# Block sums, weight sums and silu on other units, x added to the output by DMA, and another product order in an FNet and GLU kernel

## Chip, core and metric

One core of a Trainium2 chip. The metric is the time of one execution in device microseconds; of the kernel before there are three runs, median 832.66 us (832.14 to 834.09).

## What is computed

```python
x = A_x                                   # (1, 2048, 512), float32
xn = _layernorm(x, axis=-1)
# s: real part of a 2-D DFT of xn
a = jnp.einsum("bsd,ed->bse", xn, dft_hid_re)
b = jnp.einsum("bsd,ed->bse", xn, dft_hid_im)
s = jnp.einsum("ts,bse->bte", dft_seq_re, a) - jnp.einsum("ts,bse->bte", dft_seq_im, b)
# g: silu of a gated linear unit of xn, width 1792
h = _sigmoid(xn @ w_gate) * (xn @ w_up)
g = _silu(h @ w_down)
return x + s * g
```

## The kernel before

All large arrays are float32. A product of two float32 operands is made of three matmuls (`mm3`, lines 69 to 72): each operand is split into a high and a low half, and high x high (L70), high x low (L71) and low x high (L72) are summed in a PSUM bank. `split` (lines 65 to 67) makes the halves: ScalarE (ACT) copies the high one (L66), VectorE (DVE) subtracts it for the low one (L67). Every operand that TensorE (PE) reads thus costs one ACT and one DVE operation over 128 x 1024 elements.

The DFT along the sequence and that along the hidden axis are written as products of 2 x 2 blocks in seven products in place of eight. They need sums of blocks of the operands, and the seven products, numbered 1 to 7, are added up into blocks in a given order; `CHAIN` names the accumulator that a product goes on with (a, b or c), `ORDER` is the order of the products, (1, 5, 6, 3, 7, 2, 4). Sums of operand blocks are made on DVE by `combine` (L118).

All on-chip data lies in 53 equal pages of 128 x 1024 floats (`page`). The work is a list of *units* that is written out by hand. `add` puts a unit at the end of the list; `sooner(n, f)` runs f ahead of unit n, `after(n, f)` behind it. The loop at lines 979 to 991 walks the list: at unit n it first does what `sooner` has for n, then starts the loads of the units n to n+5, then makes the splits of the units n to n+2, then the unit's matmuls, then what `after` has for n. Each engine works its instructions off in that order, so this list fixes what is queued behind what on DVE, ACT, SyncE (SP, which issues loads) and GpSimd (POOL, which issues stores).

Three stages follow each other. The first (to about 425 us) makes the layer norm, the gate and up products, and most of the down products; it sums g into `g_part` in DRAM by accumulating DMAs (`gather`, L295). The change does not touch it.

The second is the product along the sequence, `seq_units`, with four columns of the result, `tc_` 0 to 3 (called column 0 to 3 below). A column has 28 units, one for each product and each of four parts `pp`; units 0 to 3 are the first product in `ORDER`, 4 to 7 the next, and so on. (Column 0 has eight units of the first stage's last down products between them.) A unit is 12 matmuls of 128 x 128 by 128 x 512. Behind the last part of a product, `after_product` copies an accumulator to a page (`snap`, ACT, L787) or joins it with a page (`join`, DVE, two operations, L794); the joins stand behind units 15, 19 and 23. The halves of an even column are stored to `f_part` (L763). The operand sums that products 5, 6, 7 and 4 need are made by `onto`, three units ahead: units 1 to 8, 13 to 16 and 21 to 24. Into this stage three kinds of work are put that later stages need:

- *block sums*: in the odd columns, `total` reads back what the even column stored (`first`), makes four sums of it and the new blocks (L118), and stores them to `f_part` (L779). For half 0 they stand behind units 20 to 23, for half 1 behind 28 to 31, that is behind units 0 to 3 of the next column or of the third stage.
- *weight sums*: four sums of the blocks of the hidden DFT's weights, `sums_ahead(n + 64, diffs, ...)`, behind units 3, 5, 6 and 8 of column 2 (DVE, L118; stored at L682).
- *silu*: `silu_ahead`, eight pages of g: load, sigmoid (ACT, L720), product (DVE, L118 called from L717), store to `gs_part` (L717), one every seven units from the end of column 0.

The third stage is the product along the hidden axis, `hidden_units`: two pairs of columns, seven products of two units each (27 units, since the very last product is one unit, `run_last`). The weights' splits are spread by hand over the units ahead (lines 851 to 855). Behind the product that ends a block (`BLOCK`: 3, 7, 2, 4), `give` multiplies it with the silu page, adds x (L882), and POOL stores it to the output (L884). `run_last` does the last block in three pieces, with products and sums on DVE (L923, L924) and stores by SP (L926); its last two pieces share one PSUM bank.

Of the kernel before, what the change touches and what calls it, by code (L numbers as in the profile page):

```python
# [12 lines left out]
ADD, SUB = ALU.add, ALU.subtract  # L13
# [18 lines left out]
def fnet_glu_kernel(ctx: ExitStack, tc: tile.TileContext, x, x_t, c_re, c_im, w_h, w_gu, w_down, out):  # L32
# [99 lines left out]
    def after(n, f):  # L132
        extra.setdefault(n, []).append(f)
# [537 lines left out]
            (b21.load, b21, b22, ADD, to[3]),  # L671
        ]

    def sums_ahead(n, make, blocks, to):

        steps = make(*blocks, to)

        def step(dst, a, b, op, to):
            at = dst()
            a, b = a.get(), b.get()  # L680
            combine(at, a, b, op)
            nc.gpsimd.dma_start(to, at)  # L682

        for i, v in enumerate(blocks):
            sooner(n + i // 2, v.load)
        for i, v in enumerate(steps):
            after(n + (3, 5, 6, 8)[i], lambda v=v: step(*v))

    def onto(a, b, op, engine, swap=False):

# [16 lines left out]
        return ops  # L707

    ORDER = (1, 5, 6, 3, 7, 2, 4)
    SLOT = {1: 0, "a": 0, 2: 1, "b": 1, 3: 2, 5: 3, 7: 4, 6: 5, 4: 6}  # L710

    def silu_ahead(n, i):
# [10 lines left out]
    def seq_units(job):  # L723
        ops = a_operands()
        left = waiting + [(job, k) for k in SEVEN]
        n = len(units)
        sums_ahead(n + 64, diffs, [Load(w_h[i, j], [4, D // 2]) for i in range(2) for j in range(2)], w_part)
        for i in range(NS // 2):
            silu_ahead(n + 28 + 7 * i, i)
        for q in range(2):  # L730
            sooner(n - 5 + q, ops[1, q].load)
            sooner(n - 3 + q, ops[1, q].get)
        for tc_ in range(NT):
            n = len(units)
            bop = {}
            for pp in range(4):
                b11, b12, b21, b22 = c_blocks(tc_, pp)
# [17 lines left out]

            first = {(half, j): Load(f_part[tc_ // 2, half, SLOT["ab"[j]]], [2, SB]) for half in range(2) for j in range(2)}

            def after_product(k, tc_=tc_, ps=ps, s=s, made=made, first=first):
                def put(blk):
                    half, j = blk // 2 ^ 1, blk % 2  # L760
                    to = f_part[tc_ // 2, half]
                    if tc_ % 2 == 0 or j:
                        nc.gpsimd.dma_start(to[SLOT["ab"[j] if tc_ % 2 == 0 else 3]], made[blk])  # L763
                    if tc_ % 2 == 0 or j == 0:
                        return
                    a0, b0 = (first[half, j].load() for j in range(2))
                    a1, b1 = made[blk - 1], made[blk]
                    t2 = []

                    def total(k):  # L770
                        if k == 6:
                            t2.append(page([2, SB], F32))
                        v = {
                            5: lambda: combine(a0, a0, a1, ADD),
                            7: lambda: combine(a1, a1, b1, ADD),
                            6: lambda: combine(t2[0], a0, b1, ADD),
                            4: lambda: combine(b0, t2[0], b0, ADD),
                        }[k]()
                        nc.gpsimd.dma_start(to[SLOT[k]], v)  # L779

                    for i, k in enumerate((5, 7, 6, 4)):
                        after(now[0] + 1 + i, lambda k=k: total(k))

                def snap(name, ch):
                    s[name] = page([2, SB], F32)
                    for d in range(2):
                        nc.scalar.activation(s[name][:, d, :], ps[ch, d], AF.Copy)  # L787
                    return s[name]

                def join(blk, name, ch, op, swap=False):  # L790
                    made[blk] = v = s[name]
                    for d in range(2):
                        x, y = v[:, d, :], ps[ch, d]
                        nc.vector.tensor_tensor(v[:, d, :], *((y, x) if swap else (x, y)), op=op)  # L794
                    put(blk)

                if k == 1:
                    snap("u1", "a")
                elif k == 5:
                    snap("u5", "c")  # L800
                elif k == 6:
                    snap("u2", "a")
                elif k == 3:
                    join(2, "u2", "c", SUB)
                elif k == 7:
                    join(3, "u5", "a", SUB, swap=True)
                elif k == 2:
                    join(0, "u1", "b", ADD)
                else:
                    made[1] = snap("u4", "a")  # L810
                    put(1)
# [19 lines left out]

            for k in ORDER:
                for pp in range(4):
                    m = len(units)
                    if (tc_ or pp > 1) and k in bop["t", pp]:
                        sooner(m - 6, bop["t", pp][k].load)
                        sooner(m - 3, bop["t", pp][k].get)
                    add([ops[k, pp // 2], bop[k, pp]], lambda k=k, pp=pp, run=run: run(k, pp))
                    if tc_ % 2 and pp == 3 and k in (7, 4):
                        for j in range(2):  # L840
                            sooner(m - 5 + 2 * j, first[0 if k == 7 else 1, j].load)
                    if left and pp % 2:
                        last_down(*left.pop(0))


    def hidden_units():
# [1 line left out]
        v1, v3, v2, v4 = (Load(w_part[i], [4, D // 2]) for i in range(4))  # L848
        a11, a12, a22 = (Load(w_h[i, j], [4, D // 2]) for i, j in ((0, 0), (0, 1), (1, 1)))
        w = {}  # L850
        for i, (k, v) in enumerate({1: a11, 5: v1, 6: v2, 3: v4, 7: v3, 2: a12, 4: a22}.items()):
            w[k] = Parts([v], v.load, [4, D // 2])
            if i < 5:
                sooner(n - 26 + 5 * i, v.load)
                sooner(n - 22 + 5 * i, w[k].get)
        CHAIN = {1: "a", 6: "a", 7: "a", 4: "a", 2: "b", 5: "c", 3: "c"}
        BLOCK = {3: (0, 1), 7: (1, 1), 2: (0, 0), 4: (1, 0)}
        for pair in range(NT // 2):
            hp = {}
            for k in ORDER:  # L860
                for half in range(2):
                    v = Load(f_part[pair, half, SLOT[k]], [2, SB])
                    hp[k, half] = Parts([v], v.load, [2, SB])
            gl, xl = ({(i, t): Load(a[(2 * pair + t) * 2 + i], [2, SB]) for i in range(2) for t in range(2)} for a in (gs_part, x_t))
            ps, s = {}, {}

            def done(k, pair=pair, gl=gl, xl=xl, ps=ps, s=s):
                def snap(name, ch):
                    s[name] = page([2, SB], F32)
                    for d in range(2):  # L870
                        nc.scalar.activation(s[name][:, d, :], ps[ch, d], AF.Copy)

                def give(ch, name=None, op=None, swap=False):
                    i, t = BLOCK[k]
                    g, xv = gl[i, t].load(), xl[i, t].load()
                    r = s[name] if name else page([2, SB], F32)
                    for d in range(2):
                        a, b = r[:, d, :] if name else g[:, d, :], ps[ch, d]
                        nc.vector.tensor_tensor(r[:, d, :], *((b, a) if swap else (a, b)), op=op or ALU.mult)
                    if name:  # L880
                        nc.vector.tensor_mul(r, r, g)
                    nc.vector.tensor_add(r, r, xv)  # L882
                    to = out[i * D // 2 : (i + 1) * D // 2, (2 * pair + t) * SB : (2 * pair + t + 1) * SB]
                    nc.gpsimd.dma_start(to.rearrange("(d p) t -> p d t", p=P), r)  # L884

                if k == 1:
                    snap("u1", "a")
                elif k == 5:
                    snap("u5", "c")
                elif k == 6:  # L890
                    snap("u2", "a")
                elif k == 3:
                    give("c", "u2", SUB, swap=True)
                elif k == 7:
                    give("a", "u5", SUB)
                elif k == 2:
                    give("b", "u1", ADD)
                else:
                    give("a")

            def run(k, half, hp=hp, ps=ps, done=done, tags=({"a": "pd", "b": "a", "c": "c"}, {"a": "b", "b": "a", "c": "c"})[pair]):
                ch = CHAIN[k]
                if k in (1, 2, 5) and half == 0:
                    for d in range(2):
# [20 lines left out]
                    row, col = (2 * i + d) * P, (2 * pair + t) * SB  # L925
                    nc.sync.dma_start(out[row : row + P, col + at.start : col + at.stop], r[:, d, at])  # L926

            for k in ORDER:
                m = len(units)
                for half in range(2):  # L930
                    sooner(m + half - 8, hp[k, half].load)
                if k in BLOCK:
                    sooner(m - 5, gl[BLOCK[k]].load)
                    sooner(m - 4, xl[BLOCK[k]].load)
                if k == 4 and pair == NT // 2 - 1:
                    add([hp[k, 0], hp[k, 1], w[k]], run_last)
                    continue
                for half in range(2):
                    add([hp[k, half], w[k]], lambda k=k, half=half, run=run: run(k, half))
# [104 lines left out]
```

## Time and profile before

| | |
|---|---|
| median of three runs | 832.66 us (832.14 to 834.09) |
| the profiled execution | 833.4 us |
| its span, first to last instruction | 831.6 us |
| PE, DVE, ACT, POOL busy | 812.3, 652.4, 491.3, 135.4 us |
| granted TensorE clock | 1.00 throughout |
| DMA | 207.27 MB, 249 GB/s on average |

The rows below and in the prediction are read like this. A group or timeline row gives the line, the engine, the operation, the tiles (written <- read), the form, the count, and in brackets the idle time of the engine ahead of it with what ended it. A row of waits reads "who <- for whom: us in all, times, longest". A row of the table by stretches gives start and end, length, then busy time and number of instructions of PE, PEld (the weight loads), DVE, ACT and POOL, the granted clock, the share of DMA engine time and the rate in GB/s. The end of a matmul is modelled: one of 128 x 512 is shown with 0.39 us.

The transfers that matter for the change, with the median from issue to landing:

```profile
g_part<-page POOLq DMA_DIRECT2D x77, 512.0 KB, 8.2
...
f_part<-page POOLq DMA_DIRECT2D x28, 512.0 KB, 6.8
...
page<-in_x_t_dram SPq DMA_DIRECT2D x8, 512.0 KB, 10.4
page<-in_w_h_dram SPq DMA_DIRECT2D x7, 512.0 KB, 9.9
out_dram<-page POOLq DMA_DIRECT2D x7, 512.0 KB, 7.7
```

### The profile page before, as it was taken

The page shows a single profiled execution, that of the slowest core. Times are in us where ns is not written, and L with a number is a line of the kernel's source. Part 1 is how long each engine was busy: PE and PEld are TensorE (multiplying, and loading weights), DVE is VectorE, ACT ScalarE, POOL GpSimd, SP SyncE. Part 2 cuts the span into 40 slices and gives each one's busy share as a digit, 9 for nine tenths or more (in the row PEclk, how much of TensorE's full clock was granted, in tenths as well). Part 3 has the DMA queues.
Part 4 walks back from the last instruction along what each step waited for, and adds up shares of the span by engine and source line. Part 5 has one row for each costly group of instructions (what it writes and reads, how often), then busy time and mean ns, then how long its engine had stood idle before and what let it go on. Part 6 is the DMA issues. An engine that isn't in the chain of part 4 may idle for free.

```text
span 831.6 us, 10507 instructions
## 1 busy us (share of the span) xinstructions
PE 812.3 (98%) x3687; PEld 673.0 (81%) x3687; DVE 652.4 (78%) x821; ACT 491.3 (59%) x762; POOL 135.4 (16%) x207
## 2 busy tenths in 40 slices
PE   8899999999999999999999999999989999999997
PEld 7888888888878888888888888888768888878786
DVE  6798867757787867776787797878898767887957
ACT  4566555654677888788877774552545245446260
POOL 2142422321111112122121100001110000011101
PEclk9999999999999999999999999999999999999999
DMA  8259998799677888989999998268965743899952
GB/s 316 107 176 392 286 273 264 189 323 302 163 172 174 227 184 194 253 211 202 291 288 291 291 326 316 69 218 270 419 250 203 277 153 127 277 360 414 413 205 102
DMA packets 58357, 207.27 MB, mean 249 GB/s; under 512 B 6592, under 2 KB 6848, under 8 KB 58304
## 3 DMA queue, kind: packets, MB, share of 16 engines
q1 hardware_dynamic: 35136, 122.70, 40.8%
q0 software_dynamic: 23168, 83.90, 39.0%
q8 instruction: 29, 0.48, 0.2%
q14 instruction: 24, 0.20, 0.1%
HBM read 122.16 MB, written 84.41 MB: 248 GB/s over the span
## 4 chain that ended last, share of the span: by engine, by line
PE 73%; issue 13%; DVE 8%; DMA 3%; ACT 2%; POOL 1%; SPq 0%; DVEq 0%; POOLq 0%
PE pd L72 6%; PE pd L71 6%; PE pd L70 6%; PE ga L71 4%; PE ga L70 4%; PE ga L72 4%; PE ua L71 4%; PE ua L72 4%; PE ua L70 4%; DVE page L67 3%; PE gc L70 3%; PE gc L71 3%; PE gc L72 3%; PE uc L71 3%; PE uc L72 3%
## 5 line engine op out<-in xcount | busy, mean ns | idle before, releaser
L67 DVE TENSOR_TENSOR page<-page 128x1024 fp32r<-128x1024 f32 (+1 forms) x340 | 320.8, 977 | 116.5 <-ACT page L66 115.8
L66 ACT ACTIVATE page<-page 128x1024 fp32r<-128x1024 f32 (+1 forms) x340 | 275.9, 859 | 108.5 <-DVE page L118 92.6
L118 DVE TENSOR_TENSOR page<-page 128x1024 f32<-128x1024 f32 (+2 forms) x184 | 167.9, 933 | 7.3 <-DMA page<-xn_part 6.5
L291 ACT ACTIVATE page<-pd 128x512 f32<-128x512 f32 x154 | 89.5, 595 | 62.2 <-PE pd L72 58.9
L295 POOL DMA_DIRECT2D g_part<-page x69 | 60.2, 903 | 276.0 <-ACT page L291 200.1
L72 PE MATMUL pd<-page 128*128 128x512 f32 x242 | 94.3, 389 | 0.6 <-DVE page L67 0.6
L71 PE MATMUL pd<-page 128*128 128x512 f32 x242 | 94.3, 389 | 0.4 <-DVE page L67 0.4
L70 PE MATMUL pd<-page 128*128 128x512 f32 x242 | 94.2, 389 | 0.0
L70 PE MATMUL ga<-page 128*128 128x512 f32 x192 | 74.9, 390 | 0.8 <-ACT page L308 0.8
L71 PE MATMUL ga<-page 128*128 128x512 f32 x192 | 75.0, 391 | 0.4 <-DVE page L67 0.4
L72 PE MATMUL ga<-page 128*128 128x512 f32 x192 | 74.8, 390 | 0.0
L71 PE MATMUL ua<-page 128*128 128x512 f32 x192 | 74.7, 389 | 0.0
L70 PE MATMUL ua<-page 128*128 128x512 f32 x192 | 74.7, 389 | 0.0
L72 PE MATMUL ua<-page 128*128 128x512 f32 x192 | 74.7, 389 | 0.0
L71 PE MATMUL gc<-page 128*128 128x512 f32 x132 | 51.6, 391 | 2.3 <-DVE page L67 2.3
L72 PEld LDWEIGHTS pd<-page 128*128 128x128 f32 x242 | 45.4, 188 | 10.3 <-DVE page L67 0.9
L71 PEld LDWEIGHTS pd<-page 128*128 128x128 f32 x242 | 45.4, 188 | 10.3 <-DVE page L67 0.8
L70 PEld LDWEIGHTS pd<-page 128*128 128x128 f32 x242 | 45.4, 188 | 9.4
L70 PE MATMUL gc<-page 128*128 128x512 f32 x132 | 51.7, 392 | 0.0
L70 PE MATMUL uc<-page 128*128 128x512 f32 x132 | 51.4, 389 | 0.0
L72 PE MATMUL uc<-page 128*128 128x512 f32 x132 | 51.4, 389 | 0.0
L72 PE MATMUL gc<-page 128*128 128x512 f32 x132 | 51.4, 389 | 0.0
(135 smaller groups left out, 1355.5 us busy)
## 6 DMA issues: line engine op xcount, KB each, us to landing
g_part<-page POOLq DMA_DIRECT2D x77, 512.0 KB, 8.2
page<-in_c_re_dram SPq DMA_DIRECT2D x36, 512.0 KB, 5.3
page<-f_part SPq DMA_DIRECT2D x36, 512.0 KB, 7.7
page<-in_c_im_dram SPq DMA_DIRECT2D x34, 512.0 KB, 6.4
page<-in_w_gu_dram SPq DMA_DIRECT2D x28, 512.0 KB, 7.4
f_part<-page POOLq DMA_DIRECT2D x28, 512.0 KB, 6.8
page<-in_w_down_dram SPq DMA_DIRECT2D x14, 512.0 KB, 9.0
page<-xn_part SPq DMA_DIRECT2D x14, 512.0 KB, 7.8
```

Of the source, the lines that this page charges most:

```text
L66: nc.scalar.activation(hi, src, AF.Copy)
L67: nc.vector.tensor_tensor(lo, src, hi.bitcast(F32), op=SUB)
L70: nc.tensor.matmul(ps, ws[0], ms[0], start=first, stop=False, skip_group_check=go_on)
L71: nc.tensor.matmul(ps, ws[0], ms[1], start=False, stop=False, skip_group_check=go_on)
L72: nc.tensor.matmul(ps, ws[1], ms[0], start=False, stop=last, skip_group_check=go_on)
L118: (engine or nc.vector).tensor_tensor(dst, a, b, op=op)
L291: nc.scalar.activation(pg[:, o, :], po, AF.Copy, scale=float(sign))
L295: nc.gpsimd.dma_start(g_part[i], pg, accum_op=ADD)
```

## The change

- The weight sums move from column 2 (behind units 3, 5, 6, 8) to column 1 (behind units 9, 10, 11, 12), with their loads at units 6 and 7.
- The silu products move to behind units 17, 18 and 20 of column 1 and 17, 18, 20, 25 and 27 of column 2.
- The block sums of half 0 move from units 20 to 23 to units 25 to 28; those of half 1 from units 28 to 31 to units 37 to 40 behind column 1 (9 to 12 of column 2) and 32 to 35 behind column 3 (4 to 7 of the third stage). The halves stored before are read back four and three units ahead of them.
- The third stage takes its products in the order (1, 2, 6, 5, 3, 7, 4), with accumulators b and c in other banks. The splits of the weights of products 1, 2, 6, 5, 3 stand behind units 9, 11, 17, 18 and 20 of column 3.
- In the third stage x is no longer loaded and added on DVE, other than for the last block. POOL copies x into the output from DRAM to DRAM in columns 2 and 3, and the block is added to it by an accumulating DMA.

No matmul is added or taken away. The diff:

```diff
-    def sums_ahead(n, make, blocks, to):
+    def sums_ahead(n, make, blocks, to, at=(3, 5, 6, 8)):
...
-            at = dst()
-            a, b = a.get(), b.get()
-            combine(at, a, b, op)
-            nc.gpsimd.dma_start(to, at)
+            v = combine(dst(), a.get(), b.get(), op)
+            nc.gpsimd.dma_start(to, v)
...
-            after(n + (3, 5, 6, 8)[i], lambda v=v: step(*v))
+            after(n + at[i], lambda v=v: step(*v))
...
     ORDER = (1, 5, 6, 3, 7, 2, 4)
+    TURNED = (1, 2, 6, 5, 3, 7, 4)
...
-        sums_ahead(n + 64, diffs, [Load(w_h[i, j], [4, D // 2]) for i in range(2) for j in range(2)], w_part)
-        for i in range(NS // 2):
-            silu_ahead(n + 28 + 7 * i, i)
+        silu = {1: (17, 18, 20), 2: (17, 18, 20, 25, 27)}
+        later = iter(range(2 * NT))
...
         for tc_ in range(NT):
             n = len(units)
+            if tc_ == 1:
+                blocks = [Load(w_h[i, j], [4, D // 2]) for i in range(2) for j in range(2)]
+                sums_ahead(n + 6, diffs, blocks, w_part, (3, 4, 5, 6))
+            for i in silu.get(tc_, ()):
+                silu_ahead(n + i - 3, next(later))
...
-                    a0, b0 = (first[half, j].load() for j in range(2))
...
                     def total(k):
+                        a0, b0 = (first[half, j].load() for j in range(2))
...
+                    at = n + 25 if half == 0 else n + 28 + (9 if tc_ < NT - 1 else 4)
+                    for j in range(2):
+                        sooner(at - 4 + j, first[half, j].load)
                     for i, k in enumerate((5, 7, 6, 4)):
-                        after(now[0] + 1 + i, lambda k=k: total(k))
+                        after(at + i, lambda k=k: total(k))
...
-                    if tc_ % 2 and pp == 3 and k in (7, 4):
-                        for j in range(2):
-                            sooner(m - 5 + 2 * j, first[0 if k == 7 else 1, j].load)
...
-        for i, (k, v) in enumerate({1: a11, 5: v1, 6: v2, 3: v4, 7: v3, 2: a12, 4: a22}.items()):
+        for i, (k, v) in enumerate({1: a11, 2: a12, 6: v2, 5: v1, 3: v4, 7: v3, 4: a22}.items()):
             w[k] = Parts([v], v.load, [4, D // 2])
             if i < 5:
-                sooner(n - 26 + 5 * i, v.load)
-                sooner(n - 22 + 5 * i, w[k].get)
+                at = n - 28 + (9, 11, 17, 18, 20)[i]
+                sooner(at - 5, v.load)
+                after(at, w[k].get)
...
+        LAST = NT // 2 - 1, 4
+
+        def place_out(pair, i, t):
+            v = out[i * D // 2 : (i + 1) * D // 2, (2 * pair + t) * SB : (2 * pair + t + 1) * SB]
+            return v.rearrange("(d p) t -> p d t", p=P)
+
+        def put_x(pair, i, t):
+
+            nc.gpsimd.dma_start(place_out(pair, i, t), x_t[(2 * pair + t) * 2 + i])
+
         for pair in range(NT // 2):
             hp = {}
-            for k in ORDER:
+            for k in TURNED:
...
+            for i, k in enumerate(TURNED):
+                if k in BLOCK and (pair, k) != LAST:
+                    after(n - 52 + 24 * pair + 3 * i, lambda pair=pair, k=k: put_x(pair, *BLOCK[k]))
...
-                    g, xv = gl[i, t].load(), xl[i, t].load()
+                    g = gl[BLOCK[k]].load()
...
-                    nc.vector.tensor_add(r, r, xv)
-                    to = out[i * D // 2 : (i + 1) * D // 2, (2 * pair + t) * SB : (2 * pair + t + 1) * SB]
-                    nc.gpsimd.dma_start(to.rearrange("(d p) t -> p d t", p=P), r)
+                    nc.gpsimd.dma_start(place_out(pair, *BLOCK[k]), r, accum_op=ADD)
...
-            def run(k, half, hp=hp, ps=ps, done=done, tags=({"a": "pd", "b": "a", "c": "c"}, {"a": "b", "b": "a", "c": "c"})[pair]):
+            def run(k, half, hp=hp, ps=ps, done=done, tags={"a": ("pd", "b")[pair], "b": "c", "c": "a"}):
...
-            for k in ORDER:
+            for k in TURNED:
...
                 if k in BLOCK:
                     sooner(m - 5, gl[BLOCK[k]].load)
+                if (pair, k) == LAST:
                     sooner(m - 4, xl[BLOCK[k]].load)
-                if k == 4 and pair == NT // 2 - 1:
                     add([hp[k, 0], hp[k, 1], w[k]], run_last)
                     continue
```

## What was predicted

> **What bounds the kernel now.** First the shares: PE 98% busy, DVE 78%, ACT 59%. Busy PE is no measure of what is left, so next the spacing of its matmuls. In the timeline two 128x512 matmuls of a row without a wait start 0.227 us apart (588.84, 589.07), though each is shown as 0.39 long. A unit of 12 matmuls takes 2.72 us, a column of 28 units 76.2 us. Now the table by stretches, cut where the accumulator of product 1 begins: the last product of column 0, columns 1, 2 and 3, and the hidden product up to its last unit.
>
> ```profile
> 500.14:511.04 10.90, 10.90 (x50) 9.01 (x48) 8.83 (x9) 3.44 (x4) 1.07 (x2) 1.00 0.87 316
> 511.04:588.84 77.80, 76.48 (x338) 63.01 (x336) 63.49 (x58) 36.72 (x41) 5.33 (x10) 1.00 0.63 221
> 588.84:668.80 79.96, 77.33 (x338) 62.77 (x336) 66.90 (x61) 35.71 (x40) 7.98 (x15) 1.00 0.73 275
> 668.80:746.58 77.78, 76.45 (x338) 63.00 (x336) 64.55 (x59) 37.49 (x42) 3.20 (x6) 1.00 0.65 223
> 746.58:819.73 73.15, 71.61 (x313) 58.39 (x312) 57.19 (x55) 34.53 (x42) 6.98 (x11) 1.00 0.77 311
> ```
>
> Column 0 runs at full rate (10.90 for 48 matmuls, 10.88 worked out). Columns 1 to 3 lose 1.6, 3.8 and 1.6 us, the hidden product 2.4 (26 units x 2.72 = 70.7). The clock (1.00) is not the cause. The waits of PE name it:
>
> ```profile
> PE gb L71 <- DVE page L67: 3.1, 3, 1.3
> PE gc L71 <- DVE page L67: 2.3, 2, 1.8
> PE ub L70 <- DVE page L923: 1.9, 1, 1.9
> ...
> PE pd L72 <- DVE page L67: 0.6, 1, 0.6
> PE pd L71 <- DVE page L67: 0.4, 1, 0.4
> PE ga L71 <- DVE page L67: 0.4, 1, 0.4
> ```
>
> Always the low half of a split (L67), the moving operand of the second matmul. Why it is late, the timeline of DVE shows, here from the end of product 7 of column 1:
>
> ```profile
> 565.64 0.69 DVE L794 TENSOR_TENSOR page<-ub,page 128x512 f32<-128x512 f32 x1
> 566.25 1.22 DVE L67 TENSOR_TENSOR page<-page 128x1024 fp32r<-128x1024 f32 x1
> 567.38 2.35 DVE L118 TENSOR_TENSOR page<-page 128x1024 f32<-128x1024 f32 x2
> 569.65 1.22 DVE L67 TENSOR_TENSOR page<-page 128x1024 fp32r<-128x1024 f32 x1
> 570.79 2.35 DVE L118 TENSOR_TENSOR page<-page 128x1024 f32<-128x1024 f32 x2
> ...
> 578.79 3.49 DVE L118 TENSOR_TENSOR page<-page 128x1024 f32<-128x1024 f32 x3
> 582.20 4.70 DVE L67 TENSOR_TENSOR page<-page 128x1024 fp32r<-128x1024 f32 x4
> ```
>
> No gap for 22 us: DVE is given three operations a unit (split, operand sum, block sum), 1.14 us each back to back, 3.4 us against PE's 2.72. So DVE bounds short stretches and has slack in the others (63 to 67 us busy of 78 to 80).
>
> **The change, part by part.** The times are those of the profiled execution: 833.4 us, span 831.6, 0.74 above the median of the runs, 832.66. All DVE operations below are 128x1024 at 1.14; a join of two is 1.3.
>
> *Where DVE has room.* Each unit has a split; units 1 to 8, 13 to 16 and 21 to 24 of a column have an operand sum too. That is 2.28 of 2.72. Units 9 to 12, 17 to 20 and 25 to 28 have only the split, so one operation more makes 2.28 there as well. The joins fall behind units 15, 19 and 23. The change puts each of its moved operations on such a unit: weight sums on 9 to 12 of column 1, silu on 17, 18, 20 (column 2 also 25, 27), block sums of half 0 on 25 to 28, of half 1 on 9 to 12 of the next column or units 4 to 7 of the hidden product, weight splits on 9, 11, 17, 18, 20 of column 3. Nothing is added to DVE.
>
> *Is a split late anywhere then?* The worst row begins with the join behind unit 15, T = its end. Join 1.3; unit 16 sum and split 3.6; unit 17 split and silu 5.9; unit 18 the same, 8.1; unit 19 split 9.3. The next join waits for PE at 10.9 and ends 12.2; unit 20 14.5; units 21 to 23 21.3; join from 21.8 to 23.1; unit 24's split, needed at unit 26, ends 25.4. PE is there at 27.2. The least margin is 1.8 us. So **the 1.6 of columns 1 and 3 and the 3.8 of column 2 go**.
>
> *Hidden product.* Today a block's end costs join or product, L881 and L882, and the splits behind it are late:
>
> ```profile
> 776.38 1.23 DVE L881 TENSOR_TENSOR page<-page 128x1024 f32<-128x1024 f32 x1
> 777.64 1.23 DVE L882 TENSOR_TENSOR page<-page 128x1024 f32<-128x1024 f32 x1
> 778.78 3.49 DVE L67 TENSOR_TENSOR page<-page 128x1024 fp32r<-128x1024 f32 x3
> ```
>
> L882 (seven times) goes; DVE then has 2.4 per block. The new order also spreads the blocks: 2 ends behind unit 3, 3 behind 9, 7 behind 11, 4 behind 13, and two weight splits move into column 3. From the end of unit 9: product 2.4, two splits 4.7 (needed at 5.4), split 5.8, product 8.2, split 9.3 (needed 10.9). **The 2.4 goes.**
>
> *The tail.* The last unit starts at E = 819.73 and PE stops at 823.9 until L923 has read the bank of its first half: 825.94, 2.06 late, because DVE does two products, L881, L882 and two more first. After: the second product of block 7 at E+0.2 to 0.9, L881 to 2.15, L923 on the finished first bank E+2.9, L924 to 4.3, L923 to 4.7. PE goes on at E+4.76 instead of E+6.21: **1.45 gained**, 0.6 of the wait stays, and all behind it (last write, E+10.7) moves with it to E+9.3.
>
> *What is added.* Seven copies of x into the output by POOL, DRAM to DRAM, 13 to 49 units (35 to 133 us) ahead of the hidden product. No row has such a copy; by the POOL issue of L884 (0.72) and a 512 KB store (L682, 2.9 to 9.8 us) they lie beside POOL's 70 idle us of each column, and the DMA share there is 0.65 to 0.73. I take 0; the upper end is 1 us, if a load of C behind one is late; below 0 there is nothing, since no wait of PE names a load. The seven x loads by SP go from a stretch where DMA is full (1.02, 414 GB/s from 746 to 785). The output writes become accumulating. Nearest rows: L295 issue 0.86, landing 5.1/8.3/11.9, against L884's 0.72 and 3.1/7.7/8.5. The last but one output then lands at E+2.5+5.1 = E+7.6 with idle DMA, 1.7 ahead of the last write, so 0. The page "DMA: Bandwidth & Descriptors" of the Trainium skill (Anatomy of one DMA — SWDGE (gpsimd) path) gives 2.0 us plus bytes by 436 GB/s, 3.2 for 512 KB: the plain store agrees (2.9), the accumulating one (5.1 at least) doesn't; by the page the margin would be 3.6, the sum the same.
>
> *New waits.* Pages. Counting lifetimes in the order of the program I find 50 to 52 of 53 pages taken in units 7 to 12 of columns 1 and 2 (now: units 1 to 9 of column 2). A page freed by a store is there only when it has landed; that such waits exist shows in SP's own waits (22.0 us on f_part stores from 560 to 760) and in this row, where DVE waits for one:
>
> ```profile
> 603.42 3.49 DVE L118 TENSOR_TENSOR page<-page 128x1024 f32<-128x1024 f32 x3 [0.23 <-DMA f_part<-page]
> ```
>
> If the page of the second block sum goes straight to the split of unit 14: sum and issue 2.65 after unit 10 starts, landing 3.1/7.4/8.7, hi and low 2.3, needed at 11.1. That is 3 us early to 2.5 late, 1.2 late by the median of L779; by the 5.8 median of 600 to 740, in time. I take 1.0 in all, nearest to today's small waits, and keep 0 to 6.
>
> Sum: 833.4 - (1.6 + 3.8 + 1.6 + 2.4 + 1.45 = 10.9) + 1.0 = 823.5; less 0.74, **822.7** as a median.
>
> **Rivals.**
> *Half of it moves* (0.20): DVE's margins of 1 to 2 us are eaten by late loads or page waits, so a stall comes back behind the joins. For it: 64 to 66 us of DVE a column stay. Against: column 0 has the same sums and loses nothing. 5.5 of 10.9 comes back: 827.2.
> *The accumulating write ends last* (0.08): if it lands over 6.8 us after issue, up to 11.9. Against: DMA share 0.10 from 800 to 820. Or one copy holds loads up. 1 to 5 us: 825.
> *Pages turn it slower* (0.06). Each crowded stretch has four stores. If all eight pages are handed straight to splits, each costs PE landing less 6.2 us. At 7.8 us that is 1.6 x 8 = 12.6, and nothing is left of the gain; at 8.7 it is 20: 842. Against: today's crowded stretch cost DVE 0.23 and ACT 1.3 on such waits. The Trainium skill's page "SBUF — State Buffer" (the "DVE blocks DMA" trap) says that a busy DVE can keep GpSimd from writing descriptors; stores would land later and this rival would win. Here a store's issue takes 0.53 under an unbroken DVE (568.89) and 0.54 beside an idle one (747.67), so I give it no more.
> *It doesn't do what it says* (0.04): the block sums that now wait for reloaded halves hold DVE as before; 832.7.
>
> **How the numbers follow.** Forecast 822.7 (0.62, own range 821.4 to 824.5: no new wait, or 2 more). The range takes in the moved half and the late write, and leaves out the last two rivals: 821.4 to 828.5. A difference under 0.2% (1.7 us) is about what a measurement here can't tell from none. Faster 0.90, same 0.04, slower 0.06.
>
> **What would show it.** Right: columns 1 to 3 of 76.2 to 77; no wait of PE for L67 over 0.5; hidden product 70.7 to 71.5; PE's wait for L923 near 0.6; no three L118 in a row at a column's end; the last write, not the accumulating one, ends the span. Wrong: PE waiting for L67 in units 10 to 17 of columns 1 or 2 with DVE or ACT waiting for f_part or w_part; SP waiting for stores ahead of the loads of C; POOL's accumulating issues far over 0.86.

## The result and the profile after

The changed kernel takes 823.88 us (median of 5 runs, 823.19 to 824.03), the one before 833.88 (5 runs, 832.14 to 834.09): a ratio of 0.9884, 95% interval 0.987 to 0.9898. The profiled execution took 823.88 us with a span of 822.1, that is 9.5 us less than the profiled execution before.

The table by stretches of the changed kernel, cut at the same places as in the prediction (columns 1, 2 and 3, then the third stage up to its last unit; the columns are the same too):

```profile
510.84:587.00 76.16, 76.16 (x338) 63.11 (x336) 65.87 (x60) 35.84 (x40) 5.86 (x11) 1.00 0.68 238
587.00:663.16 76.16, 76.16 (x338) 63.10 (x336) 66.07 (x60) 37.91 (x42) 10.42 (x18) 1.00 0.76 279
663.16:739.32 76.16, 76.16 (x338) 63.12 (x336) 63.52 (x58) 37.38 (x42) 4.82 (x8) 1.00 0.74 268
739.32:811.13 71.81, 70.97 (x313) 58.53 (x312) 52.73 (x51) 34.48 (x42) 11.01 (x13) 1.00 0.85 284
```

All three columns take 76.16 us, and PE is busy for 76.16 of them: nothing is left to gain there. DVE is as busy as before (65.9, 66.1 and 63.5 us against 63.5, 66.9 and 64.6). So the work was not made less, it was laid where there is room. The third stage takes 71.81 where 26 full units are 70.7. The rest is in the waits of PE, of which these two lie behind column 0:

```profile
PE pd L70 <- DVE page L895: 0.8, 1, 0.8
...
PE ub L70 <- DVE page L937: 0.5, 1, 0.5
```

No wait for a split (L67) is left. The second row is the rest of the wait in the last unit (L923 is L937 now). The first is new: L70 is the *first* matmul of a triple, so it is not a low half that is late, and L895 is the first operation of `give`, which reads an accumulator. The timelines of DVE and of PE at that place:

```profile
768.73 3.49 DVE L67 TENSOR_TENSOR page<-page 128x1024 fp32r<-128x1024 f32 x3
772.13 1.28 DVE L895 TENSOR_TENSOR page<-page,pd 128x512 f32<-128x512 f32 x2
```
```profile
771.73 0.39 PE L72 MATMUL pd<-page 128*128 128x512 f32 x1
772.96 0.47 PE L70 MATMUL pd<-page 128*128 128x512 f32 x1 [0.84 <-DVE page L895]
```

Product 7 of the first pair starts its last matmul at 771.73 in the two banks `pd`. Product 4 goes on adding in the same banks, and DVE, busy with three splits, has not read them yet. In the old order product 2 stood between the two. From start to start the stall is 1.23 us in place of 0.23.

The gain, by the cuts: 1.6 + 3.8 + 1.6 in the columns, 1.3 in the third stage (73.15 to 71.81), 0.9 from the start of the last unit to the end of the span (11.88 to 10.98), and 0.2 ahead of column 1, mostly work that the change doesn't touch. Together 9.5.

### The profile page after: what moved, and what is told of

Its sections match the earlier page's. It is cut to its first block, busy times and chain, and to the rows that moved or that the text cites. A ratio compares the mean times of both kernels' runs of the same rounds, so it can differ in the third digit from the quotient of the medians.

```text
span 822.1 us, 10472 instructions
## 1 busy us (share of the span) xinstructions
PE 810.6 (99%) x3687; PEld 674.6 (82%) x3687; DVE 645.1 (78%) x814; ACT 491.2 (60%) x762; POOL 144.0 (18%) x214
## 4 chain that ended last, share of the span: by engine, by line
PE 93%; DVE 4%; ACT 2%; issue 1%; POOL 0%; DVEq 0%
PE pd L70 6%; PE pd L71 6%; PE pd L72 6%; PE ga L70 5%; PE ga L71 5%; PE ua L72 5%; PE ga L72 5%; PE ua L71 5%; PE ua L70 5%; PE gc L71 3%; PE uc L70 3%; PE gc L70 3%; PE uc L72 3%; PE gc L72 3%; PE uc L71 3%; PE gb L70 3%
## 5 line engine op out<-in xcount | busy, mean ns | idle before, releaser
L67 DVE TENSOR_TENSOR page<-page 128x1024 fp32r<-128x1024 f32 (+1 forms) x340 | 322.1, 979 | 117.0 <-ACT page L66 115.5
L66 ACT ACTIVATE page<-page 128x1024 fp32r<-128x1024 f32 (+1 forms) x340 | 276.1, 859 | 91.6 <-DVE page L118 69.0
L118 DVE TENSOR_TENSOR page<-page 128x1024 f32<-128x1024 f32 (+2 forms) x184 | 169.3, 935 | 8.5 <-DMA page<-xn_part 6.4
L70 PE MATMUL pd<-page 128*128 128x512 f32 x242 | 94.4, 390 | 0.8 <-DVE page L895 0.8
L72 PE MATMUL pd<-page 128*128 128x512 f32 x242 | 94.3, 390 | 0.0
L70 PE MATMUL ga<-page 128*128 128x512 f32 x200 | 78.2, 391 | 0.8 <-ACT page L308 0.8
L72 PE MATMUL ga<-page 128*128 128x512 f32 x200 | 78.0, 390 | 0.0
L72 PE MATMUL ua<-page 128*128 128x512 f32 x200 | 78.0, 390 | 0.0
L71 PE MATMUL ga<-page 128*128 128x512 f32 x200 | 78.0, 390 | 0.0
L71 PE MATMUL ua<-page 128*128 128x512 f32 x200 | 78.0, 390 | 0.0
L70 PE MATMUL ua<-page 128*128 128x512 f32 x200 | 77.9, 390 | 0.0
L70 PEld LDWEIGHTS pd<-page 128*128 128x128 f32 x242 | 45.5, 188 | 10.6 <-issue 1.2
L72 PEld LDWEIGHTS pd<-page 128*128 128x128 f32 x242 | 45.5, 188 | 9.3
L70 PE MATMUL ub<-page 128*128 128x512 f32 (+1 forms) x126 | 48.3, 384 | 0.5 <-DVE page L937 0.5
L70 PE MATMUL gc<-page 128*128 128x512 f32 x124 | 48.7, 392 | 0.0
L71 PE MATMUL gc<-page 128*128 128x512 f32 x124 | 48.3, 390 | 0.0
L72 PE MATMUL gc<-page 128*128 128x512 f32 x124 | 48.3, 390 | 0.0
L70 PE MATMUL uc<-page 128*128 128x512 f32 x124 | 48.3, 390 | 0.0
```

The source lines that it names most:

```text
L66: nc.scalar.activation(hi, src, AF.Copy)
L67: nc.vector.tensor_tensor(lo, src, hi.bitcast(F32), op=SUB)
L70: nc.tensor.matmul(ps, ws[0], ms[0], start=first, stop=False, skip_group_check=go_on)
L71: nc.tensor.matmul(ps, ws[0], ms[1], start=False, stop=False, skip_group_check=go_on)
L72: nc.tensor.matmul(ps, ws[1], ms[0], start=False, stop=last, skip_group_check=go_on)
L118: (engine or nc.vector).tensor_tensor(dst, a, b, op=op)
```

## Experiments

Twelve kernels were run, each beside the kernel before on the same chip; the ratios are to that one (its median was 833.2, 834.1 and 833.6 us in the three groups).

### The second stage alone

The second stage is that of the changed kernel, `hidden_units` whole that of the kernel before; against the changed kernel:

```diff
-            for k in TURNED:
+            for k in ORDER:
...
+                    nc.vector.tensor_add(r, r, xv)
...
-                    nc.gpsimd.dma_start(place_out(pair, *BLOCK[k]), r, accum_op=ADD)
+                    nc.gpsimd.dma_start(to.rearrange("(d p) t -> p d t", p=P), r)
...
-                at = n - 28 + (9, 11, 17, 18, 20)[i]
-                sooner(at - 5, v.load)
-                after(at, w[k].get)
+                sooner(n - 26 + 5 * i, v.load)
+                sooner(n - 22 + 5 * i, w[k].get)
```

> The moves of the second stage alone; the third stage as in the kernel before. If each column's loss is its own crowded DVE stretch, columns 1 to 3 take 76.2 us each (before 77.8, 80.0, 77.8) and the third stage keeps its 73.2 us to its last unit and its 2.1 us wait at the end: 833.9 - 7.0 = 826.9. Rival: the third stage's weight splits, which here still stand at their old places in column 3, need the other part of the change too; then column 3 stays near 77 to 78 and the time is 828 to 829.

Measured: 827.78 us, 0.9935 (0.9918 to 0.9951).

```profile
510.31:586.47 76.16, 76.16 (x338) 63.08 (x336) 65.87 (x60) 35.84 (x40) 5.86 (x11) 1.00 0.66 231
586.47:662.63 76.16, 76.16 (x338) 63.08 (x336) 66.15 (x60) 37.79 (x42) 7.45 (x14) 1.00 0.73 261
662.63:738.79 76.16, 76.16 (x338) 63.08 (x336) 63.22 (x58) 37.44 (x42) 2.65 (x5) 1.00 0.65 230
738.79:813.22 74.43, 72.17 (x314) 58.35 (x313) 58.54 (x57) 34.64 (x42) 8.07 (x13) 1.00 0.81 330
```

The columns are full with the old third stage behind them; the rival falls. But the third stage got 1.3 us slower (73.15 to 74.43). The four block sums of its units 4 to 7 (L118 at 752.59, 754.86, 758.03 and 764.02) now stand around the sums of its first finished block (760.3 to 764.1), and DVE has a gap of 0.81 us ahead of 756.89 and then none up to 786.5; at the same place of the kernel before (764.67) the gap was 3.08 us. So the parts are not independent: 7.0 gained, 1.3 given back.

### x by DMA alone

```diff
-                    nc.vector.tensor_add(r, r, xv)
...
-                    nc.gpsimd.dma_start(to.rearrange("(d p) t -> p d t", p=P), r)
+                    nc.gpsimd.dma_start(place_out(pair, i, t), r, accum_op=ADD)
```

with `put_x` as in the changed kernel and x loaded for the last block alone, in the old product order, the second stage as before but for the copies.

> Only x by copies and accumulating DMAs; product order, block sums, weight sums and silu as before. Theory: the sum L882 alone made the third stage late, so without it the old order has no wait of PE for a split there (70.7 to 71.2 us in place of 73.2), and the last unit's wait falls from 2.1 to 0.7 us, with the last store landing late beside an accumulating one (gain 0.9 in all at the end): 833.9 - 2.4 - 0.9 = 830.6. Rival: the new product order is needed for it; then the third stage stays above 72 us and the time is 832 or more.

Measured: 830.42 us, 0.9959 (0.9946 to 0.9972). The third stage runs at full rate in the old order:

```profile
746.77:817.49 70.72, 70.72 (x313) 58.58 (x312) 51.33 (x50) 34.42 (x42) 9.86 (x11) 1.00 0.84 274
```

Taking seven L882 off DVE is enough for the 2.4 us. (The edit takes seven x loads out of this stage too; that it is not they is argued from the timeline in the prediction, where DVE works without a gap ahead of the late splits.) The last unit up to the end of the span takes 11.15 us (11.88 before).

### The product order alone

```diff
-            for k in ORDER:
+            for k in TURNED:
...
-tags=({"a": "pd", "b": "a", "c": "c"}, {"a": "b", "b": "a", "c": "c"})[pair]
+tags={"a": ("pd", "b")[pair], "b": "c", "c": "a"}
```

and the same order in the list of the weight splits.

> Only the new product order of the third stage with its banks; x still added on DVE, the rest as before. Theory: product 4 goes on in the bank that the end of product 7 has still to read on DVE, and with L882 in the queue DVE is later there than after the whole change (1.0 us): 1 to 3 us of wait at the first matmul of product 4 of the first pair (L70, for the first operation of give); the end as before or longer. 832.5 to 835. Rival: the order by itself spreads the blocks and removes the 2.4 us: 831.5.

Measured: 832.79 us, 0.9997 (0.9987 to 1.0006), no difference. The profiled execution is the slowest of the ten (835.14 us), and a part of its third stage is a fallen clock (0.98, last section). That stage takes 76.05 us, no split is waited for in it, and the longest wait is that for the accumulator:

```profile
746.70:822.75 76.05, 73.08 (x313) 59.39 (x312) 58.91 (x57) 34.47 (x42) 7.00 (x11) 0.98 0.74 296
```
```profile
PE pd L70 <- DVE page L880: 2.1, 1, 2.1
```

(L880 is the first operation of `give` in this kernel.) 1.3 us of it come back after the last unit has started (10.62 against 11.88 us); that part of DVE's queue now lies ahead of that start is a likely reason, not a shown one. By itself the new order gains nothing.

### Products 7 and 3 exchanged

```diff
-    TURNED = (1, 2, 6, 5, 3, 7, 4)
+    TURNED = (1, 2, 6, 5, 7, 3, 4)
```

and the same in the list of the weight splits.

> The whole change with products 7 and 3 exchanged in the third stage, so that product 3 (accumulator c) stands between 7 and 4 (both accumulator a). Theory (a wait for a bank): the 0.84 us idle of PE at the first matmul of product 4 (1.0 us of start to start) goes, third stage to its last unit 70.8 us (71.8 before the exchange): 823.9 - 1.0 = 822.9. Rival (DVE is simply late there, whatever bank): the wait comes back as a wait for a split (L67) or in product 3, and the time stays at 823.9.

Measured: 822.68 us (822.36 to 822.99), 0.9869 (0.9854 to 0.9884). Its waits of PE have no L895, and its third stage is full:

```profile
739.00:809.72 70.72, 70.72 (x313) 58.58 (x312) 52.63 (x51) 34.48 (x42) 11.02 (x13) 1.00 0.86 290
```

DVE is as late as before at the end of unit 11 (L895 at 771.81, behind three splits), but what it reads there is product 3's accumulator, and product 4 goes on in another one. The rival falls. The four runs all lie below those of the changed kernel, but the two were not run side by side and the intervals of their ratios overlap; what the traces show is the 1.1 us of the third stage.

### The last two weight splits early

```diff
-            if i < 5:
-                at = n - 28 + (9, 11, 17, 18, 20)[i]
+            if True:
+                at = n - 28 + (9, 10, 11, 12, 17, 18, 20)[i]
```

> The whole change in its own product order, but the weight splits of products 7 and 4 too stand in column 3 (units 9, 10, 11, 12, 17, 18, 20 for the seven). Theory: product 4's first matmul waits for the bank only because DVE comes 0.3 us late to the end of product 7, behind the split of the weights of 4; two operations less, and the read of the bank is done while PE works on: no wait, 71.8 to 70.8 us, 822.9. Rival (product 4 right behind 7 in one bank waits whatever DVE's queue): 823.9.

Measured: 822.72 us, 0.9868 (0.9851 to 0.9884); third stage 70.72 us, no wait for L895.

```profile
770.95 0.68 DVE L895 TENSOR_TENSOR page<-page,pd 128x512 f32<-128x512 f32 x1
772.25 0.69 DVE L895 TENSOR_TENSOR page<-page,pd 128x512 f32<-128x512 f32 x1 [0.62 <-PE pd L72]
```

DVE reads the first bank at 770.95, 1.1 us ahead of the start of product 4 (772.06), while PE works in the second; it now waits for PE and not PE for it. So the stall needs both: the same accumulator in two products behind each other, and a DVE queue that is late at that moment.

### Block sums at their old places

```diff
-                    at = n + 25 if half == 0 else n + 28 + (9 if tc_ < NT - 1 else 4)
+                    at = n + 20 if half == 0 else n + 28
```

with the loads of the halves stored before at their old places too.

> The whole change, but the block sums at their old places (behind units 20 to 23 and 28 to 31, with their old loads). Theory: on units 21 to 24 an operand sum stands already, so columns 1 and 3 lose 1 to 1.6 us each again, column 2 (sums beside operand sums on units 0 to 3, but no weight sums and no silu there now) 0 to 1, the third stage 0 to 0.5: 823.9 + 2 to 4.7, likeliest 827. Rival: silu and weight sums made the stretches crowded and the block sums alone fit: 824.

Measured: 827.44 us, 0.9928 (0.9913 to 0.9943).

```profile
510.07:588.54 78.47, 76.80 (x337) 62.91 (x336) 66.75 (x61) 35.88 (x40) 6.92 (x13) 1.00 0.69 253
588.54:664.98 76.44, 76.44 (x338) 62.99 (x336) 64.73 (x59) 38.09 (x42) 9.36 (x16) 1.00 0.71 252
664.98:742.76 77.78, 76.45 (x338) 62.98 (x336) 64.48 (x59) 37.37 (x42) 5.88 (x10) 1.00 0.76 283
```

Columns 1 and 3 lose 2.3 and 1.6 us, column 2 only 0.3. In columns 1 and 3 PE waits for a split again:

```profile
PE gb L71 <- DVE page L67: 2.9, 2, 1.6
```

### Weight sums, then silu, at their old places

```diff
-            if tc_ == 1:
+            if tc_ == 2:
...
-                sums_ahead(n + 6, diffs, blocks, w_part, (3, 4, 5, 6))
+                sums_ahead(n, diffs, blocks, w_part)
```

> The whole change, but the weight sums at their old places (behind units 3, 5, 6, 8 of column 2). Theory: units 3 to 8 then hold 2.28 x 6 + 4 x 1.14 = 18.2 us of DVE work against 16.3 of PE, 1.9 over, about the margin of two units that a split has: column 2 loses 0 to 1 us, the rest nothing: 823.9 to 824.9. Rival: the weight sums were the main cause of column 2's 3.8 us: 826 or more.

Measured: 824.06 us, 0.9884 (0.9867 to 0.99); column 2 takes 76.44 us, the others 76.16.

```diff
-        silu = {1: (17, 18, 20), 2: (17, 18, 20, 25, 27)}
+        silu = {0: (31,), 1: (2, 9, 16, 23), 2: (2, 9, 16)}
```

> The whole change, but the eight silu products at their old places, one every seven units (behind 31 of column 0; 2, 9, 16, 23 of column 1; 2, 9, 16 of column 2). Theory: each is one operation of 1.14 us, alone or beside one other, and the queue is behind by 0.7 to 1.4 us at most: nothing lost, 823.9; at unit 23 of column 1, behind a join and ahead of the block sums, 0 to 0.5. Rival: silu on crowded units was a third of the loss: 826.

Measured: 823.75 us, 0.9883 (0.9868 to 0.9898); all columns 76.16 us. Undone alone, neither of these two moves changes the time by anything that can be measured.

### Block sums and weight sums at their old places

The edits of the block sums and of the weight sums above, together.

> The whole change, but the block sums and the weight sums both at their old places; silu and the third stage as changed. Alone the block sums cost column 2 0.3 us and the weight sums 0.3 us. Theory (queue length): together they stand on units 0 to 8 of column 2 in one row, 9 splits, 8 operand sums, 4 and 4 = 25 operations, 28.5 us against 24.5 of PE, so the loss is not 0.6 but 2.5 to 4: 829.5 to 831. Rival (each has its own price): 827.7.

Measured: 829.24 us, 0.9948 (0.9933 to 0.9962).

```profile
510.93:588.71 77.78, 76.45 (x338) 62.99 (x336) 62.47 (x57) 36.00 (x40) 4.80 (x9) 1.00 0.58 201
588.71:667.19 78.48, 76.98 (x337) 62.84 (x336) 69.19 (x63) 37.84 (x42) 11.49 (x20) 1.00 0.84 307
```

Column 2 loses 2.3 us, where the two alone lost 0.3 each: the price is not a sum of prices. That it is what a stretch of queue has over PE's time (4.0 us here, 28.5 less 24.5), less the lead that the splits have, fits; the lead was not measured, and the loss is a little under the 2.5 to 4 that the theory gave. In the kernel before, where silu stands at its old places as well, it is 3.8.

### Fewer pages

The second of the two with 51:

```diff
-PAGES = 53
+PAGES = 48
```

> The whole change with 48 pages in place of 53, the fewest with which the program can run at all. Theory: a page is handed on two units after it is freed at the earliest; with five spare pages gone, splits wait for the PE or a store that frees their page, and columns 1 and 2 lose several us in units 7 to 13: 828 to 840. Rival: pages never bind, the loads and splits have slack enough: within 1 us of 823.9.

> The whole change with 51 pages in place of 53 (48 cost 33 us in columns 1 and 2). Theory (spare pages give a freed page time): three spare pages are half of the five, a split then waits a unit less for its page; a loss of 0 to 6 us, 824 to 830. Rival (a cliff at the last page alone): 823.9.

Measured: 857.43 us with 48 pages, 1.0289 (1.0263 to 1.0314), and 824.8 with 51, 0.9894 (0.9879 to 0.9909). Columns 1 and 2, first with 48, then with 51 pages:

```profile
510.06:604.92 94.86, 85.70 (x337) 67.10 (x336) 65.12 (x60) 36.31 (x40) 5.86 (x11) 0.93 0.51 181
604.92:697.49 92.57, 81.74 (x337) 63.24 (x336) 65.82 (x60) 38.50 (x42) 10.43 (x18) 0.98 0.62 227
```
```profile
510.51:586.96 76.45, 76.45 (x337) 63.00 (x336) 65.75 (x60) 35.80 (x40) 5.86 (x11) 1.00 0.64 226
586.96:663.61 76.65, 76.50 (x338) 63.00 (x336) 66.06 (x60) 38.12 (x42) 10.42 (x18) 1.00 0.75 279
```

With 48 both columns lose 16 to 19 us, with 51 they lose 0.3 and 0.5, with 53 nothing. The spare pages decide, and steeply. With 48 the waits that the prediction feared are there, but they are the smaller part: between 510 and 697 us five rows of ACT and DVE name a store, 12.8 us in all, while in five rows of L66 ACT waits 62.4 us for PE to free a page. A part of the loss is the clock (0.93 and 0.98, last section). The largest row of each kind:

```profile
ACT page L66 <- PE uc L71: 18.3, 5, 5.5
...
ACT page L66 <- DMA f_part<-page: 4.0, 1, 4.0
```

### No x in the stored blocks

```diff
-                    nc.gpsimd.dma_start(place_out(pair, *BLOCK[k]), r, accum_op=ADD)
+                    nc.gpsimd.dma_start(place_out(pair, *BLOCK[k]), r)
```

This kernel leaves x out of seven blocks of the output.

> The whole change, but the seven blocks are stored by plain DMAs in place of accumulating ones: x is left out of the sum there, the output is s times g alone. Theory: the accumulating write of the last but one block holds up the last stores; with a plain one the last store lands 1.9 us after its issue in place of 2.4, and the stretch from the start of the last unit to the end of the span is 10.5 us in place of 11.0. Rival: the stores are slow for another reason; 11.0.

One execution, 823.55 us, which lies among the runs of the changed kernel. The stretch from the start of the last unit to the end of the span is 10.45 us (changed kernel 10.98). The landing times of the last three stores, first in the changed kernel, then in this one:

```profile
L940 SPq DMA_DIRECT2D out_dram<-page x3: 332/337/337, 815.5 to 818.6; - x3
...
DMA to landing us min/median/max: 2.4/4.4/5.1
```
```profile
L940 SPq DMA_DIRECT2D out_dram<-page x3: 332/338/338, 815.7 to 818.8; - x3
...
DMA to landing us min/median/max: 1.9/1.9/2.1
```

The accumulating write of the last but one block is issued at 813.57 and lands 5.9 us later; the plain one in its place lands in 3.2. While it is under way, the first small store behind it takes 5.1 us in place of 2.1.

## Why the prediction was right, and where not

- **The number.** 823.88 is 1.2 above the forecast of 822.7 and inside its own range (821.4 to 824.5). In the profiled executions 9.9 us were to go and 9.5 went. Some of that is luck: the 1.0 set aside for pages, which cost nothing, stands against 1.1 and 0.5 us that were not foreseen. That the medians fell by just 10.0 is luck too, since the median before rose by 1.2 with two more runs.
- **The bound.** Right: DVE's queue in short stretches, not its total. The three columns came out at 76.16 us, the 76.2 that was worked out from the spacing of matmuls, and the terms 1.6, 3.8 and 1.6 were gained in full.
- **Which moves.** Not told apart in the prediction. Undoing the block sums' move alone loses 4.2 of the 7.0 us (2.3 + 0.3 + 1.6), undoing that of the weight sums 0.3 and that of silu 0; but beside the old block sums in column 2, weight sums at their old places make 0.3 into 2.3, and with silu too it is the 3.8 of the kernel before.
- **The hidden product, 2.4.** The cause was right: without L882 it is gone (70.72 in the old order). But the step "from the end of unit 9" failed in the new order. It had DVE start to read the end of product 7 at 5.8 us (5.6 came out), when PE is through with product 7 at 5.4, and asked of that only whether the next split is in time; that the matmuls of product 4 need the accumulator which DVE reads from 5.8 on was left out. That read is 0.84 us of wait, 1.1 us of the stretch. Two experiments removed it in different ways, and both gave 70.72. Whether the new order is needed beside the moved block sums, and what the new places of the weight splits are worth, was not run.
- **The tail, 1.45.** On PE and DVE right: from the start of the last unit to the last matmul 6.24 us (before 7.63), a gain of 1.39, with 0.5 us of wait left (0.6 said). But the last write did not move with it: it landed at E+9.9 (E is the start of the last unit) and not at E+9.3. It was counted as 0 that the accumulating write is still under way; it does not end last, yet it slows the stores beside it, and 0.5 is lost. With plain stores the last write lands at E+9.3. The prediction had the row by which accumulating stores take longer (5.1 us at the least, plain ones 3.1), and used it only for where that write itself ends.
- **New waits, 1.0 for pages.** Wrong in kind, and about right in size by luck. Pages cost nothing in columns 1 and 2; the 1.0 came from the accumulator's wait. The count of 50 to 52 pages taken was too high, since the program runs with 48.
- **Rivals.** "Half of it moves" and "pages turn it slower" did not come. The second is between two and five pages away: 51 pages cost 0.8 us in the columns, 48 make the kernel slower. (Its 1.6 x 8 is 12.8, not 12.6.) Stores were not held up by a busy DVE: PE waits for nothing in the columns, POOL's f_part stores still take 0.53 us to issue, and those of the block sums land in 7.5 us in the median (7.4 before). The trap that the prediction took from the Trainium skill ("SBUF — State Buffer", the "DVE blocks DMA" trap) is narrower on its page: it holds while DVE runs an operation in a two-port mode, a condition that the prediction left out.
- **POOL and copies.** The seven copies (0.71 us of POOL each) landed in 7.2 to 13.7 us, and no wait of PE in the columns followed; the accumulating issues took 1.18 to 1.24, over the 0.86 of the nearest row. That row writes whole rows of 4 KB, the output has rows of 2 KB; plain stores show the same step (0.53 for `f_part`, 0.72 for the output), but that the rows are the reason was not tested.
- **Its own signs.** Two came out against it: the hidden product took 71.81 us (70.7 to 71.5 said), and the accumulating issues were far over 0.86. One reading was too broad: of the rows called "always the low half of a split, the moving operand", L923 is no split, and at L72 it is the low half of the stationary operand that is late.

## What to carry to other kernels

Where PE is nearly always busy, look for the engine that feeds it by stretches and not by its total: write down for each unit of PE's time what is in the feeder's queue, and move what is not urgent to units with a free place. Such moves had no price of their own here: the same operations were free in one company and cost a microsecond or more in another, because the queue as a whole was late. And when the order of products is changed, go through the accumulators: a product that goes on in a bank right behind the one whose end must be read out from it puts the reader's lateness on PE.

## What the runs showed of the hardware

**The granted clock fell after waits of 2 us, and among many shorter ones.** In two kernels with the old column 2 (x by DMA alone, order alone) that column took 80.9 and 80.8 us and not the 80.0 of the kernel before, though its waits of PE sum to no more (2.5 and 2.4 us, before 2.7). The table for x by DMA alone, around its 2.0 us wait:

```profile
606.00:608.00 2.00, 0.39 (x2) 0.35 (x3) 2.00 (x3) 1.06 (x1) 0.11 (x1) 1.00 1.03 422
608.00:610.00 2.00, 2.00 (x8) 1.55 (x7) 2.00 (x3) 1.06 (x1) 0.00 (x0) 0.70 0.91 342
610.00:612.00 2.00, 2.00 (x7) 1.54 (x6) 2.00 (x2) 0.00 (x0) 0.53 (x1) 0.50 0.60 234
612.00:614.00 2.00, 2.00 (x10) 1.67 (x9) 2.00 (x3) 1.06 (x1) 0.00 (x0) 0.95 0.64 264
```

Behind the wait the clock is 0.50 for about 3.4 us (608.8 to 612.2), and in that time matmuls start 0.43 us apart in place of 0.23. The profiled execution of the kernel before had a wait of 1.8 us at the same place and kept 1.00. In the order alone the same happened once more behind the 2.1 us wait for the accumulator. With 48 pages the clock was at 0.77 on average from 538 to 568, where no single wait of PE is over 1.1 us but PE is idle for 7.8 of the 30. So a wait near 2 us can cost about 0.9 us more than it lasts, in some executions. The page "TensorE: Matmul & The Clock Gate" of the Trainium skill advises to have no idle gap of more than about 3 us (Why this matters for your kernels), and names a window of 3.4 us (What's actually happening). The length of the slow stretch agrees with that window; but here a single wait of 2.0 us, with one of 0.4 us some 5 us ahead of it, was enough. The spread of the kernel before (832.1 to 835.3 over all its runs) goes with the clock: beside the experiments, 13 executions at a mean clock of 1.00 took 832.7 to 833.5 us, 15 at 0.994 to 0.997 took 833.2 to 835.3. Where in these the clock fell is not on record, so that such waits are the cause is likely, but not shown.

**PE waits for a bank while DVE reads another part of it.** The last piece of the last unit waits 0.5 us for DVE's read of other columns of the same bank (1.9 us in the kernel before, where DVE was later). The page "PSUM — Partial Sum Buffer" of the Trainium skill (PSUM bank collisions raise a hardware error) says that two engines on one bank collide also at disjoint columns, so that the program must order them. No run here lets the two collide; the row of the wait shows what the order costs.
